# A transformer block on one core: order of the Q/K/V stage's x hand-over, halos, weight loads and first LN2 changed

## The chip, the cores and the metric

One Trainium2 chip, one core of it. The core has a matmul engine (TensorE, PE in the profile, with its weight loads as PEld), a vector engine (VectorE, DVE), a scalar engine (ScalarE, ACT), a general engine (GpSimd, POOL) and SyncE (SP), which here only issues DMAs. Each engine works through its own instructions in order and meets the others through semaphores. The metric is device time of one execution in microseconds (us). The kernel before took 362.25 us, the median of three executions (361.2 to 363.64).

## What is computed

A pre-LayerNorm block on x of 2048 rows by 576 columns, in bf16:

```python
qkv = LN(x) @ wqkv                      # 32 heads of 18 columns
logits[s, w] = q[s] . k[s - 2 w] / sqrt(18)      # w = 0..7, masked where s < 2 w
o = sum_w softmax(logits)[s, w] * v[s - 2 w]
h = x + o @ wo
out = h + gelu(LN(h) @ w1 + b1) @ w2 + b2        # w1: 576 x 4608, w2: 4608 x 576
```

## The kernel before

The 2048 rows are 16 tiles of 128; row `16 p + j` lies in tile j on partition p. So the rows that attention needs (2, 4, ... rows back) lie in tiles of the same parity on the same partition, and, where a tile number would fall under 0, in a tile of that parity one partition further down. All K and V of a parity stand in one ring, `kv_ring[parity]`, one slot a tile. Tiles are attended in falling order (`ATT_ORDER`, in the code `A`: 14, 12, ..., 0, 15, 13, ..., 1). When tile j has been attended to, its slot is replaced by the same tile moved down one partition, for the tiles that come after: `store_halo` (L306) writes the slot to `kv_dram`, `halo(j, 1)` (K) and `halo(j, 2)` (V, both L347) read it back moved. `halo(j, 1)` must follow the QK products of j and precede those of the next tile; `halo(j, 2)` does the same for the products with V.

The order of the work on PE, ACT, DVE, SP and POOL is written out by hand: what the Python code emits first, an engine does first.

**The Q/K/V stage, 24 visits.** `seq` lists 48 duos (tile, K or V or Q); visit `qd` takes duos 2 qd and 2 qd + 1. A duo (`qkv_duo`, matmuls at L228) runs in two phases, since each matmul uses half the array's rows and two run side by side: 10 matmuls in the first, 8 in the second. `visit` runs the first phase of every duo, then a hook, then the second phases, each followed by the duo's evacuation on ACT (L322) and by what `between` lists. Before a second phase starts, a no-op on POOL (`marker`, L238) must have seen the end of that duo's first phase. The duos use three PSUM buffers in turn (A, B, C), so a duo's first matmul waits for the evacuation of the duo three before. A fourth, D, serves the transposes and the duos with Wo. After each visit come `after[qd]` and `loads[qd]`. Visits 0 to 11 do K, Q and V of the even tiles, whose x is transposed on PE (`tr_x`); visits 12 to 23 do the odd tiles O0 to O7 (1, 3, ..., 15), three visits for a pair: V12 is K and V of O0, V13 Q of O0 and K of O1, V14 V and Q of O1, and so on; V21 is the first that reads the last pair, O6 and O7.

**x of the odd tiles** goes by DRAM. `ln1_act` (L174, ACT) normalizes a tile into `q_all`; `out_x(i)` (L292, L293, SP) stores pair i to `xd`; `in_x(i)` (L296, SP) reads it back transposed into `xnT`. A buffer of `xnT` (5 in all) is used again once the visits that read it are done.

**Attention of the first two tiles** (A[0] = 14, A[1] = 12) runs on DVE beside these visits: `att_qk_a` (L352: products), `att_qk_add` (L361: four folding adds), L368 to L375 (logits, maximum), `att_exp` on ACT, `att_den`, `att_pv` (L401 to L414), which leaves o in `q_all`. `o_tail` (L199, ACT) copies its last 64 columns twice, `tr_o` transposes it on PE (L182) into D, ACT copies it to `oT` (L434), and `wo_duo` multiplies by Wo as a third duo of a visit (`wo_with`). Then LN2: `ln2` adds x and takes statistics (L473, L148, L149, L155, L487, DVE), `ln2_rstd` raises to the power -0.5 (L161, POOL), `ln2_norm` (L539, L174, ACT) normalizes, `tr_h` transposes on PE (L188, L192), and ACT copies into `hnT` (L557). With both tiles in `hnT`, the MLP of group 0 starts.

**The MLP, 8 groups of two tiles.** For each group PE does `hn @ w1` (`pm`, L228, gelu on ACT, L584), Wo of the next group (`pw`), and the product with w2 (`po`, L603 for groups 0 and 1, L691 for the rest). Beside it DVE does attention and ACT and POOL LN2 of the next group. In group 0, attention of A[2] and A[3] is finished, `pv_t` sends o through DRAM (L210, L211, and the transposing read L216) to `oT`, and Wo of A[3] runs as a visit inserted at row 19 of the first w2 tile.

**Weight loads** (`load`, L104) wait for the last ACT evacuation before them (`pace`). `load_w1(c)` is a sixth of W1 (768 KB), `load_wo([q])` a quarter of Wo, `load_w2(n)` 3, 4 or 7 of W2's 36 row blocks of 144 KB. All go through SP's queue, in which an instruction that waits holds up those behind it; the loads' queue places are therefore set by the visit at which they are listed.

**Start.** 13 matmuls on constants (`busy`, L833) keep PE at work while the first x tile comes; then `tr_x` of the first tile and visit 0.

Of the kernel before, what the change touches and what calls it, by code (L numbers as in the profile page):

```python
# [17 lines left out]
def kernel(  # L18
# [12 lines left out]
    nc = tc.nc  # L31
    P = 128
    _, S, D = A_x.shape
# [57 lines left out]
    b2_bc = x_all[:, ODD[-1], :]  # L91
# [4 lines left out]
    def psum_pair(tag, name, dtype=F32):  # L96
        n = 512 if dtype == F32 else 1024
        return psum.tile([P, 2, n], dtype, tag=f"ps{tag}", name=name)
# [119 lines left out]
    def half_rows(r):  # L218
        return slice(r * HP, (r + 1) * HP)
# [51 lines left out]
    def new_xnT(js):  # L271
        t = qp.tile([P, KT, 2 * P], BF16, tag="xnT", name="xnT", bufs=5)
        for n, j in enumerate(js):
            xnT[j] = t[:, :, n * P:(n + 1) * P]
        return t

    def tr_x(j, tag):
        pair = psum_pair(tag or "CAB"[(ring_pos[0] + 1) % 3], "xt_pt")
        transpose_in(pair, q_all[:, j, :])
        if EVEN.index(j) % 2 == 0:  # L280
            new_xnT(EVEN[EVEN.index(j):][:2])
        for k0, k1 in ((0, 2), (2, KT)) if j in EVEN[0:2] else ((0, KT),):
            nc.scalar.copy(**turned(xnT[j], pair, k0, k1))
# [57 lines left out]
    def logit_of(js):  # L341
        return logits[:, sides(js)]
# [15 lines left out]
    def att_qk_add(j, steps):  # L358
        for o, a, c in steps:
            n = (c - a if c < 9 else 9) * H  # L360
            nc.vector.tensor_tensor(out=prod[:, :, o * H:o * H + n], in0=prod[:, :, a * H:a * H + n],  # L361
                                    in1=prod[:, :, c * H:c * H + n], op=ALU.add)

    def att_qk_b(j, i, skip=0):
        side[j] = i
        out = logit_of([j])[:, 0]
        att_qk_add(j, ((0, 0, 9), (0, 0, 4), (0, 0, 2), (0, 0, 1))[skip:])
        nc.vector.tensor_tensor(out=out, in0=prod[:, :, 0:H], in1=prod[:, :, 8 * H:9 * H], op=ALU.add)  # L368
        if j // 2 + 1 < W:
            nc.vector.memset(out[0:1, j // 2 + 1:W, :], -1e9)  # L370
# [332 lines left out]
    def c_(fn, *a):  # L703
        return lambda: fn(*a)
# [96 lines left out]
    def call(fns):  # L801
        for fn in fns:
            fn()

    with tc.manual_schedule(engines={ENG.PE, ENG.Activation, ENG.DVE, ENG.SP, ENG.Pool}):
# [23 lines left out]
        load_w1h()  # L829
        busy = psum_pair("D", "busy")  # L830
        ones = nc.const_aps.tensor(1.0, [P, 512], BF16)
        for n in [512] * 8 + [P] * 5:
            nc.tensor.matmul(busy[:, 0, 0:n], lhsT=ones[:, 0:P], rhs=ones[:, 0:n], start=True, stop=True)  # L833
        nc.gpsimd.memset(mhalf[:], -0.5)
        nc.gpsimd.memset(eps2[:], EPS * EPS)
# [63 lines left out]
        A = ATT_ORDER  # L899
# [35 lines left out]
            ln2_ins(c, d)  # L935

        loads = {}
        for c, v in enumerate((2, 3, 4, 13, 13, 17)):
            loads[v] = loads.get(v, []) + [c_(load_w1, c)]
        for q, v in enumerate((6, 8, 11, 12)):  # L940
            loads[v] = [c_(load_wo, [q])]
        for n, v in enumerate((19, 19, 20, 20, 21, 22)):
            loads[v] = loads.get(v, []) + [c_(load_w2, n)]
        after = {
            0: [c_(ln1_even, 3), c_(ln1_even, 4)],
            1: [c_(ln1_even_rstd, 2, 3), c_(ln1_even, 5)],
# [6 lines left out]
            8: [c_(att_qk_a, A[1]), c_(att_qk_rest, A[1], 1), c_(ln1_act, 8, 3), c_(out_x, 1),  # L953
                c_(store_halo, A[1]), c_(store_halo, A[0], slice(1, 2))],
            9: [c_(ln1_act, 9, 0)],
            10: [c_(att_pv, A[0]), c_(ln1_act, 9, 1), c_(in_x, 1), c_(halo, A[1], 1)],
            11: [c_(out_x, 2), c_(halo, A[0], 2)],
            12: [c_(ln1_act, 10, 0)],
            13: [c_(ln1_act, 10, 1), c_(in_x, 2), c_(out_x, 3), c_(store_halo, A[2]), c_(store_halo, A[3])],
            14: [c_(att_pv, A[1]), c_(in_x, 3), c_(load, b2_bc, B_b2.partition_broadcast(P))],  # L960
            15: [c_(halo, A[1], 2), c_(o_tail, A[0])],
            17: [c_(o_tail, A[1]), c_(ln2, A[0]), c_(att_qk_a, A[2])],
            18: [c_(ln2_rstd, A[0]), c_(halo, A[2], 1)],
            19: [c_(ln2, A[1])],
            20: [c_(ln2_rstd, A[1]), c_(att_qk_rest, A[2], 0)],
        }
        between = {
            10: [c_(att_exp, A[0])],
            13: [c_(att_exp, A[1])],
            18: {1: [c_(tr_o, A[1], "D")]},  # L970
            19: {1: [c_(ln2_norm, A[0])]},
            21: [c_(ln2_norm, A[1])],
            22: [c_(att_exp, A[2])],
        }
        wo_with = {17: A[0], 19: A[1]}
        hooks = {
            0: {1: lambda: call([c_(tr_x, EVEN[1], "C"), c_(ln1_even, 2)])},
            **{n: {m: c_(tr_x, EVEN[2 * n + m - 1], "D" if m == 1 else None) for m in (1, 2)} for n in (1, 2, 3)},
            12: c_(tr_b1, "D"),
            16: c_(tr_o, A[0], "D"),  # L980
            21: c_(tr_h, A[0], "D"),
            22: c_(tr_h, A[1], "D"),
        }
        seq = [(j, t) for t in (1, 2) for j in EVEN[:2]] + [(j, 1) for j in EVEN[2:]] \
            + [(j, 0) for j in A[0:2]] + [(j, 2) for j in EVEN[2:]] + [(j, 0) for n in (0, 4, 2) for j in EVEN[n:n + 2]] \
# [1 line left out]

        ln1_even_rstd(0, 1)
        tr_x(EVEN[0], "D")
        for qd in range(len(seq) // 2):  # L990
            duos = [qkv_duo(*seq[2 * qd]), qkv_duo(*seq[2 * qd + 1])]
            if qd in wo_with:
                duos.append(wo_duo(wo_with[qd], "D"))
            visit(duos, hooks.get(qd), between.get(qd, ()), apart=qd == 0)
            call(after.get(qd, ()))
            call(loads.get(qd, ()))
# [34 lines left out]
        p, q, r, s = "ABDC"  # L1031

        gelu_table()
        for k, g in enumerate(GROUPS):
            c, d = GROUPS[k + 1] if k + 1 < len(GROUPS) else (None, None)
# [87 lines left out]
            if 3 <= k < 7:  # L1123
                mlp2_fast(g, rows, (s, p, q, r), wo, x, True)
                p, q, r, s = q, r, p, s
            else:
                mlp2_fast(g, rows, (q, p, r, s), wo, x)
                p, q, r, s = r, s, p, q
# [30 lines left out]
```

## Time and profile before

| | |
|---|---|
| median of three executions | 362.25 us (361.2 to 363.64) |
| the profiled execution, its own time | 362.23 us |
| its span, first to last instruction | 360.4 us |
| PE / DVE / ACT / POOL busy | 352.6 / 295.9 / 235.9 / 48.1 us |
| mean granted TensorE clock | 0.995 |

| stretch, us from the span's start | what | PE busy | DVE busy | ACT busy |
|---|---|---|---|---|
| 0 to 35.80 | start, visits 0 to 11 | 33.28 | 30.23 | 27.33 |
| 35.80 to 68.15 | visits 12 to 23 | 30.33 | 30.62 | 21.85 |
| 68.15 to 106.31 | MLP group 0 | 38.16 | 34.33 | 29.08 |
| 106.31 to 144.12 | MLP group 1 | 37.81 | 35.93 | 24.13 |
| 144.12 to 323.60 | MLP groups 2 to 6 | 179.48 | 155.02 | 118.77 |
| 323.60 to 360.40 | MLP group 7, last stores | 33.50 | 9.73 | 14.74 |

How to read it: a timeline line gives start, duration, engine, source line, operation, what is written from what, count, and in brackets the idle time of that engine ahead of it with what ended the wait. Starts of neighbouring instructions can overlap, since an engine takes up the next one before the last has drained. The DMA column of a page gives no times on an engine: SP's lines are the issue of a DMA, and its landing comes later.

### The profile page before, as it was taken

What the parts mean: (1) busy time and instruction counts of PE and PEld (TensorE: products, weight loads), DVE (VectorE), ACT (ScalarE), POOL (GpSimd) and SP (SyncE); (2) the same over time, 40 slices, a digit from 0 to 9 for tenths busy, and PEclk for the clock granted to TensorE, in tenths of its full rate; (3) what the DMA queues carried; (4) which work ended last, traced back from release to release, by engine and by line L of the source; (5) the groups of instructions that cost most, each with busy time, mean ns of one, the idle gap of its engine ahead of it and who ended that gap; (6) DMA issues with size and microseconds to landing.
All of it is one profiled execution on the core that took longest, in us unless ns stands there. A gap on an engine that the chain in (4) does not pass through costs nothing.

```text
span 360.4 us, 11550 instructions
## 1 busy us (share of the span) xinstructions
PE 352.6 (98%) x4938; PEld 290.7 (81%) x4938; DVE 295.9 (82%) x416; ACT 235.9 (65%) x524; POOL 48.1 (13%) x61
## 2 busy tenths in 40 slices
PE   7999998999999999999999999999999999999996
PEld 3788886788778877887788778877887788778874
DVE  5999999989889998998799899989998989520431
ACT  4889764898556783668656956695669566706620
POOL 2340005000212020201110202021102110210000
PEclk8999999999999999999999999999999999999999
DMA  7996599972636496732463355344545254283001
GB/s 240 329 294 193 147 258 310 367 253 55 169 66 100 132 244 109 129 79 51 91 102 90 85 124 84 90 86 120 88 90 99 58 85 58 54 120 51 4 1 34
DMA packets 63492, 46.29 MB, mean 128 GB/s; under 512 B 32192, under 2 KB 61760, under 8 KB 63440
## 3 DMA queue, kind: packets, MB, share of 16 engines
q1 hardware_dynamic: 59472, 41.50, 43.6%
q0 software_dynamic: 3744, 3.84, 9.9%
q8 instruction: 38, 0.62, 0.8%
q10 hardware_dynamic: 224, 0.22, 0.3%
q14 instruction: 14, 0.11, 0.1%
HBM read 23.38 MB, written 12.42 MB: 99 GB/s over the span
## 4 chain that ended last, share of the span: by engine, by line
PE 80%; DVE 11%; DMA 5%; ACT 2%; issue 1%; SPq 0%; DVEq 0%; ACTq 0%
PE pm L228 39%; PE po L691 25%; PE po L603 10%; PE pw L228 4%; DMA xnT<-xd 3%; DVE ln_stats L148 2%; DVE prod L361 2%; DVE prod L407 1%; DVE prod L352 1%; PE pq L228 1%; DMA x_all<-in_A_x_dram 1%; DMA wq_sb<-in_A_wqkv_dram 1%; ACT h_all L584 1%; DVE prod L413 1%; DVE ln_mv L149 1%
## 5 line engine op out<-in xcount | busy, mean ns | idle before, releaser
L228 PE MATMUL pm<-hnT,w_sb 64*128 64x256 bf16 x2304 | 143.0, 269 | 0.0
L584 ACT ACTIVATE h_all<-pm,b_sb 128x256 f16<-128x256 f32 (+1 forms) x288 | 108.7, 496 | 51.0 <-PE pm L228 50.3
L228 PEld LDWEIGHTS <-w_sb 64*128 64x128 bf16 x2304 | 111.6, 94 | 15.2 <-issue 1.7
L228 PE MATMUL pq<-wq_sb,xnT 64*128 64x288 bf16 x720 | 55.7, 286 | 3.0 <-DMA xnT<-xd 1.8
L691 PEld LDWEIGHTS <-h_all 128*128 128x128 f16 x480 | 46.2, 98 | 13.7 <-issue 1.6
L228 PEld LDWEIGHTS <-xnT 64*128 64x128 bf16 x864 | 44.7, 95 | 11.9 <-DMA xnT<-xd 2.1
L361 DVE TENSOR_TENSOR prod<-prod 128x2304 bf16<-128x2304 bf16 (+1 forms) x64 | 44.2, 691 | 2.1
L352 DVE TENSOR_TENSOR prod<-kv_ring,q_all 128x4608 bf16<-128x4608 bf16 x16 | 40.8, 2551 | 3.2 <-POOL ln_rstd L498 2.4
L407 DVE TENSOR_TENSOR prod<-kv_ring,probs 128x4608 bf16<-128x4608 bf16 x16 | 40.9, 2558 | 2.2 <-DMA kv_ring<-kv_dram 1.7
L228 PE MATMUL pm<-hnT,w1h_sb 64*128 64x256 bf16 x288 | 39.2, 269 | 0.0
L691 PE MATMUL po<-w2a_sb,h_all 128*128 128x288 bf16 (+1 forms) x262 | 35.9, 286 | 0.0
L413 DVE TENSOR_TENSOR prod<-prod 128x2304 bf16<-128x2304 bf16 (+1 forms) x32 | 33.9, 1058 | 1.1
L603 PEld LDWEIGHTS <-h_all 128*128 128x128 bf16 x288 | 27.9, 98 | 7.9 <-issue 0.9
L691 PEld LDWEIGHTS <-kv_ring 128*128 128x128 f16 x252 | 24.6, 98 | 6.3
L603 PE MATMUL po<-w2a_sb,h_all 128*128 128x288 bf16 x224 | 28.5, 286 | 0.0
L228 PE MATMUL pq<-wqh_sb,xnT 64*128 64x288 bf16 x144 | 28.1, 288 | 0.0
L793 POOL DMA_DIRECT2D x_all<-o_sb x12 | 10.7, 888 | 125.1 <-PE pw L228 72.3
L498 POOL TENSOR_TENSOR ln_rstd<-ln_var,mhalf 128x1 f32<-128x1 f32 x13 | 10.2, 786 | 84.2 <-ACT ln_var L497 84.2
L161 POOL TENSOR_TENSOR ln_rstd<-ln_veps,mhalf 128x1 f32<-128x1 f32 (+2 forms) x14 | 14.1, 1019 | 45.4 <-DVE ln_nmean L487 28.0
L691 PE MATMUL po<-w2b_sb,h_all 128*128 128x288 bf16 (+1 forms) x122 | 19.7, 286 | 0.2 <-DVE h_all L671 0.2
L228 PE MATMUL pw<-wo_sb,oT 64*128 64x288 bf16 x256 | 19.5, 283 | 0.0
L671 DVE TENSOR_TENSOR kv_ring<-h_all 128x1536 f16<-128x1536 f16 (+3 forms) x9 | 6.8, 760 | 15.4 <-ACT h_all L584 15.3
(113 smaller groups left out, 400.3 us busy)
## 6 DMA issues: line engine op xcount, KB each, us to landing
w_sb<-in_B_w_dram SPq DMA_DIRECT2D x6, 768.0 KB, 6.3
kv_ring<-kv_dram SPq DMA_DIRECT2D x28, 144.0 KB, 2.4
kv_dram<-kv_ring SPq DMA_DIRECT2D x13, 288.0 KB, 4.3
x_all<-in_B_b_dram SPq DMA_DIRECT2D x15, 144.0 KB, 3.8
w2a_sb<-in_B_w_dram SPq DMA_DIRECT2D x2, 1008.0 KB, 7.1
td<-q_all SPq DMA_DIRECT2D x14, 144.0 KB, 2.3
td<-hn SPq DMA_DIRECT2D x14, 144.0 KB, 1.8
x_all<-h POOLq DMA_DIRECT2D x14, 144.0 KB, 4.5
```

Of the source, the lines that this page charges most:

```text
L148: nc.vector.bn_stats(out=stats[:, i, c, :], in_=src[:, c * HALF:(c + 1) * HALF])
L161: nc.gpsimd.tensor_tensor(out=rstd[:], in0=veps[:], in1=mhalf[:].to_broadcast([P, n]), op=ALU.pow)
L228: last = nc.tensor.matmul(duo["g"][r ^ swap][i], lhsT=lhsT, rhs=rhs, start=(swap == 0 and i == 0 and kt == 0), stop=(swap == 1 and kt == K ...
L352: ins = nc.vector.tensor_tensor(out=prod[:], in0=k_ring[j % 2], in1=q_all[:, j, :].unsqueeze(1) .to_broadcast([P, W, D]), op=ALU.mult).ins
L361: nc.vector.tensor_tensor(out=prod[:, :, o * H:o * H + n], in0=prod[:, :, a * H:a * H + n], in1=prod[:, :, c * H:c * H + n], op=ALU.add)
L407: nc.vector.tensor_tensor(out=prod[:].rearrange("p w (d h) -> p w d h", h=H), in0=v_ring[j % 2].rearrange("p w (d h) -> p w d h", h=H), in ...
L413: nc.vector.tensor_tensor(out=prod[:, 0:n, :], in0=prod[:, 0:n, :], in1=prod[:, n:2 * n, :], op=ALU.add)
L498: ins = nc.gpsimd.tensor_tensor(out=rstd[:], in0=var[:], in1=mhalf[:], op=ALU.pow).ins
L584: pace[0] = nc.scalar.activation(out=hT(grp)[:, f, 0:N], in_=ps[:, r, i * N:(i + 1) * N], func=ACT.Gelu_apprx_tanh, bias=b1_sb[:, f:f + 1] ...
L603: nc.tensor.matmul(banks[half], lhsT=hT(grp)[:, f, i * P:(i + 1) * P], rhs=w2_rows(f)[:, half * HALF:(half + 1) * HALF], start=(f == 0), s ...
L691: nc.tensor.matmul(bank, lhsT=l, rhs=r, start=start, stop=stop, skip_group_check=True)
L793: nc.gpsimd.dma_start(out=x_of(j), in_=o_of.pop(j), accum_op=ALU.add)
```

## The change

Nothing of the computation changes; the work per engine is the same but for 15 more matmuls on constants, and the order of these pieces is other:

```diff
-        for n in [512] * 8 + [P] * 5:
+        for n in [512] * 8 + [P] * 8:
             nc.tensor.matmul(busy[:, 0, 0:n], lhsT=ones[:, 0:P], rhs=ones[:, 0:n], start=True, stop=True)
...
-        for c, v in enumerate((2, 3, 4, 13, 13, 17)):
-            loads[v] = loads.get(v, []) + [c_(load_w1, c)]
-        for q, v in enumerate((6, 8, 11, 12)):
-            loads[v] = [c_(load_wo, [q])]
-        for n, v in enumerate((19, 19, 20, 20, 21, 22)):
-            loads[v] = loads.get(v, []) + [c_(load_w2, n)]
+        for v, fns in ((2, [(load_w1, 0)]), (3, [(load_w1, 1)]), (4, [(load_w1, 2)]), (6, [(load_wo, [0, 1])]), (8, [(load_wo, [2])]),
+                       (11, [(load_wo, [3])]), (14, [(load_w1, 4), (load_w1, 5)]), (15, [(load_w2, 0)]), (16, [(load_w2, 1)]),
+                       (17, [(load_w2, 2)]), (18, [(load_w2, 3)]), (20, [(load_w2, 4)]), (21, [(load_w2, 5)])):
+            loads[v] = [c_(*fn) for fn in fns]
...
-            10: [c_(att_pv, A[0]), c_(ln1_act, 9, 1), c_(in_x, 1), c_(halo, A[1], 1)],
-            11: [c_(out_x, 2), c_(halo, A[0], 2)],
-            12: [c_(ln1_act, 10, 0)],
-            13: [c_(ln1_act, 10, 1), c_(in_x, 2), c_(out_x, 3), c_(store_halo, A[2]), c_(store_halo, A[3])],
-            14: [c_(att_pv, A[1]), c_(in_x, 3), c_(load, b2_bc, B_b2.partition_broadcast(P))],
-            15: [c_(halo, A[1], 2), c_(o_tail, A[0])],
-            17: [c_(o_tail, A[1]), c_(ln2, A[0]), c_(att_qk_a, A[2])],
-            18: [c_(ln2_rstd, A[0]), c_(halo, A[2], 1)],
-            19: [c_(ln2, A[1])],
-            20: [c_(ln2_rstd, A[1]), c_(att_qk_rest, A[2], 0)],
+            10: [c_(att_pv, A[0]), c_(ln1_act, 9, 1), c_(out_x, 2), c_(in_x, 1), c_(halo, A[1], 1), c_(load_w1, 3)],
+            11: [c_(ln1_act, 10, 0)],
+            12: [c_(ln1_act, 10, 1), c_(out_x, 3), c_(in_x, 2)],
+            13: [c_(halo, A[0], 2), c_(in_x, 3), c_(store_halo, A[2]), c_(store_halo, A[3])],
+            14: [c_(att_pv, A[1]), c_(load, b2_bc, B_b2.partition_broadcast(P))],
+            15: [c_(o_tail, A[0])],
+            16: [c_(halo, A[1], 2)],
+            17: [c_(ln2, A[0]), c_(att_qk_a, A[2])],
+            18: [c_(att_qk_add, A[2], ADDS[:2])],
+            19: [c_(halo, A[2], 1)],
+            20: [c_(ln2, A[1]), c_(att_qk_rest, A[2], 0, 2)],
...
         between = {
...
-            18: {1: [c_(tr_o, A[1], "D")]},
-            19: {1: [c_(ln2_norm, A[0])]},
-            21: [c_(ln2_norm, A[1])],
+            18: [c_(o_tail, A[1])],
+            19: {0: [c_(ln2_rstd, A[0])], 1: [c_(ln2_norm, A[0])]},
+            21: {0: [c_(ln2_rstd, A[1])], 1: [c_(ln2_norm, A[1])]},
...
-        wo_with = {17: A[0], 19: A[1]}
+        wo_with = {17: A[0], 20: A[1]}
...
-            21: c_(tr_h, A[0], "D"),
-            22: c_(tr_h, A[1], "D"),
+            19: c_(tr_o, A[1], "D"),
+            22: c_(tr_h, A[0], "D"),
+            23: c_(tr_h, A[1], "D"),
...
         tr_x(EVEN[0], "D")
+        busy = psum_pair("B", "busy")
+        for n in range(12):
+            sl = half_rows(n % 2)
+            nc.tensor.matmul(busy[:, n % 2, 0:P], lhsT=ones[sl, 0:P], rhs=ones[sl, 0:P], start=True, stop=True)
```

`ADDS` is the list of the four folding adds of `att_qk_add`. In words: the last odd pair's x is normalized after V11 and V12 (before: V12 and V13), stored after V12 (V13) and read after V13 (V14), and both come ahead of the V halo of A[0] or of the two K/V stores where they stood behind them. Of W1, sixth 3 moves from V13 to V10, sixth 4 from V13 to V14 and sixth 5 from V17 to V14. W2's six pieces move from V19 to V22 to V15 to V21, so that four of them stand ahead of the K halo of A[2] in SP's queue. Of Wo, quarter 1 moves from V8 to V6, 2 from V11 to V8, 3 from V12 to V11. The transposes of o of A[1] move from the end of V18 to the middle of V19, its Wo duo from V19 to V20, its LN2 statistics from after V19 to after V20, and DVE does two of A[2]'s folding adds ahead of them. The two LN2 powers on POOL are emitted behind the markers of V19 and V21 (before: ahead of them). The transposes of h move from V21 and V22 to V22 and V23.

More of the change, by code (lines that the diff above doesn't have):

```diff
@@ L362, in att_qk_add @@
                                     in1=prod[:, :, c * H:c * H + n], op=ALU.add)
+    ADDS = ((0, 0, 9), (0, 0, 4), (0, 0, 2), (0, 0, 1))
     def att_qk_b(j, i, skip=0):
@@ L366, in att_qk_b @@
         out = logit_of([j])[:, 0]
-        att_qk_add(j, ((0, 0, 9), (0, 0, 4), (0, 0, 2), (0, 0, 1))[skip:])
+        att_qk_add(j, ADDS[skip:])
         nc.vector.tensor_tensor(out=out, in0=prod[:, :, 0:H], in1=prod[:, :, 8 * H:9 * H], op=ALU.add)
```

## The prediction

> **What bounds the kernel now.** First the page's busy line: PE is busy for 352.6 of 360.4 us, so all that can be won is in its few waits.
>
> ```profile
> PE 352.6 (98%) x4938; PEld 290.7 (81%) x4938; DVE 295.9 (82%) x416; ACT 235.9 (65%) x524; POOL 48.1 (13%) x61
> ```
>
> Then PE's waits, whole span: nothing of size after the Q/K/V stage, and one large wait in it.
>
> ```profile
> PE pq L228 <- DMA xnT<-xd: 1.8, 1, 1.8
> PE pq L228 <- DMA wq_sb<-in_A_wqkv_dram: 1.1, 2, 0.7
> ```
>
> Its place is in the chain of waits (start, us, what): the read of the last pair, issued at 51.01, landed only at 60.40, and V21 needs it at 58.5. Behind it the chain goes over LN2 of A[1]: V22's `tr_h` waits for hn.
>
> ```profile
> 51.01 9.39 DMA xnT<-xd
> ...
> 60.44 1.40 PE pq L228 x20
> ...
> 63.64 0.88 ACT hn L174
> ...
> 64.56 0.29 PE h_pt L188 x8
> ```
>
> Third, the timeline around the two hand-overs of o to PE. Here DVE, not PE, sets the pace: o of A[0] is ready at 45.51, its tail copy at 45.84, and PE comes at 45.90. For A[1] PE has finished at 52.53 and starts at 52.85.
>
> ```profile
> 45.05 0.46 DVE L414 TENSOR_TENSOR q_all<-prod 128x576 bf16<-128x576 bf16 x1
> ...
> 45.54 0.30 ACT L199 COPY tail<-q_all 128x128 bf16<-128x128 bf16 x1
> ...
> 45.90 0.28 PE L182 MATMUL o_pt<-ident,q_all 64*128 64x64 bf16 x8
> ```
>
> Fourth, the granted clock (us, busy of PE, PEld, DVE, ACT, POOL, clock, DMA): PE runs at half clock from 6.93 to 10.33.
>
> ```profile
> 3.52:6.93 3.41, 1.78 (x25) 1.07 (x24) 2.67 (x10) 1.53 (x4) 0.56 (x2) 1.00 0.98 319
> 58.13:61.54 3.41, 1.66 (x28) 1.12 (x25) 3.20 (x9) 1.29 (x3) 1.66 (x1) 1.00 1.06 351
> 6.93:10.33 3.40, 3.29 (x38) 1.85 (x35) 2.71 (x8) 1.50 (x3) 0.52 (x1) 0.50 1.08 351
> ```
>
> Last, DVE's and POOL's timeline. DVE has no gap from 24 us to 63 us; then it waits twice for a halo, and PE meets DVE's product again at 91.80, where Wo of A[3] needs oT.
>
> ```profile
> 63.60 2.56 DVE L352 TENSOR_TENSOR prod<-kv_ring,q_all 128x4608 bf16<-128x4608 bf16 x1 [0.47 <-DMA kv_ring<-kv_dram]
> ```
> ```profile
> 79.77 2.56 DVE L407 TENSOR_TENSOR prod<-kv_ring,probs 128x4608 bf16<-128x4608 bf16 x1 [0.97 <-DMA kv_ring<-kv_dram]
> ```
> ```profile
> 91.80 0.48 PEld L228 LDWEIGHTS <-oT 64*128 64x128 bf16 x10 [0.24 <-DMA oT<-td]
> ```
> ```profile
> 54.17 2.86 POOL L161 TENSOR_TENSOR ln_rstd<-ln_veps,mhalf 128x1 f32<-128x1 f32 x1 [26.38 <-DVE ln_nmean L487]
> 58.65 1.66 POOL L161 TENSOR_TENSOR ln_rstd<-ln_veps,mhalf 128x1 f32<-128x1 f32 x1 [1.62 <-DVE ln_nmean L487]
> ```
>
> **Part 1, constants at the start.** The first run of `busy` ends at 4.30 and PE then waits until 4.83: three more of 128 columns cost a quarter of a 512-column one each (0.43 us apart), 0.11, so 0.32 in a gap of 0.53. The twelve run in six pairs, 0.64 us at half clock, in the gap from 5.15 to 5.87. Cost 0; were both gaps gone, 0.96. They may keep the clock up. A stretch with 1.78 us PE busy of 3.41 lost the clock, one with 1.66 kept it; but the first holds many short transposes whose drain counts as busy. Streaming alone I estimate at 1.2 us for it (0.6 `busy`, 0.13 transposes, 0.48 pq) and 1.5 for the second. With 15 more, at least 0.16 + 0.32 = 0.48 at full clock, the first has 1.7, so I take the clock as kept: 3.4 x 0.5 = 1.7 us sooner on PE at 10.33. That goes into a wait: V16 meets o of A[0] at 45.90, which is DVE's chain, without a gap since 24 us and before that bound to x. Worth 0 on the path (ends: 0 and 1.7).
> The Trainium skill (TensorE: Matmul & The Clock Gate, Part 1) lets the clock fall only after an idle window of about 3.4 us. The 3.40 us at half clock agree in length; that the window before was half busy does not. By that rule the 15 matmuls would change nothing, and the sum would be the same.
>
> **Part 2, x of the last pair.** On ACT two `ln1_act` (0.87 each) go one visit earlier. The first now stands ahead of V12's evacuations, so V13's second duo waits about 0.1 at 38.7, inside the meeting with DVE. `out_x(3)` issues at about 40.4 instead of 46.63. `halo(A0, 2)` waits for DVE until 42.79 and now no longer holds up the last quarter of Wo, `out_x(3)` and `in_x(2)`, only `in_x(3)`, which issues at about 44.1 when its store has landed (3 us). It lands by 48 at 3.7 us, the median of these four, by 54 at its old 9.39; needed at 58.2. So 58.51 to 60.44, 1.93 us, goes whole. `in_x(1)` is pushed behind `out_x(2)` to about 37.1, lands at 40.8, needed at 42.5. The K/V stores (4.2 us) are needed at 56.6 only.
>
> **Part 3, A[1] a visit on.** A visit takes 2.20 us (first phases at 18.79, 20.99, 23.20), a Wo duo 1.10, `tr_o` 0.14, `tr_h` 0.38. `tr_o` in the middle of V19 falls at 53.75, after o (52.13) and the tail (52.46): the 0.32 us at 52.53 goes. Then V20 starts at 54.88, with Wo until 58.2, V21 58.2, V22 60.5. DVE does two folding adds first (1.37 + 0.70), so LN2 of A[1] runs from 58.62, not 56.53, its last result comes at 60.7. Total DVE work until 63.12 is unchanged.
> The powers behind the markers: before, V19's first marker stood behind a power until 54.13, needed at 54.83. Worth 0 (ends 0 and 0.1, the marker's lateness against its need if PE comes sooner). Now V20's and V22's markers stand behind the powers, but are not needed before 56.7 and 62.1, and the powers can start at 54.17 and 60.7. What is new is ACT's order: norm of A[1], hnT of A[0], V22's evacuations. The power of A[1] starts at 60.7. Its price is unknown: spans of 2.86, 1.66 and 0.67 (at 91.67), longer the longer the DVE operation beside it (2.48, 1.37, 0.42). Beside it now are adds of 0.43 and 0.30: I take 0.8, between 0.67 and 1.66 but nearest the 0.67. Then 61.5; nmean and hn 1.2, 62.7; hnT 0.65; V22's first evacuation 0.6, 63.95. V23's second duo wants that buffer at 63.7: waits 0.3. `tr_h` of A[1] in V23 then finds hn ready (0.29 of the old wait gone). V21's second duo waits 0.1 for an evacuation behind norm of A[0].
> PE reaches the MLP at 68.15 - 0.32 - 1.93 - 0.29 + 0.3 + 0.1 = 66.0, 2.1 us sooner. With a power of 1.66 it is 1.2; with 2.86, 0.1.
>
> **Part 4, loads and halos.** W2's first four pieces, W1's last two, b2 and two stores, 4.5 MB, are now queued between 45.5 and 53.6, ahead of `halo(A2, 1)` at 56.6. At the 260 to 380 GB/s that the windows of 5 us from 50 to 70 show they take 12 to 17 us: with 0.4 for itself the halo lands at 59 (it cannot before, at 2.4 after issue) to 63 instead of 63.58, DVE wants it at 63.12: 0.47 won. Behind the waiting halos in SP's queue stand W2's second piece (`halo(A1, 2)`, until 49.5) and its last two (`halo(A2, 1)`, until 56.6), which are not used before 87 us: 0. W1's sixth 3, now at about 39, shares the engines with `in_x(1)` and `out_x(3)`; W1's fourth and fifth are used behind 72, and come sooner or as soon. Wo's quarters come two or three visits sooner and are used at 48.25: 0. The V halo of A[2], issued at 74.79 behind W2's last pieces, took 4.88; those pieces are now through by about 73, so it takes some 2.4 (page: median) and 0.97 is won. DVE comes 1.44 sooner. oT of A[3]: transposed read issued at 88.74 plus 2.92 is 91.66, so now 90.2; PE wants it at 91.80 - 2.1 = 89.7. It waits 0.5. (If the store ahead of that read took 2.6 as its twin and not 3.66, no wait.)
>
> **Sum.** 2.1 - 0.5 = 1.6 us. From 92 us on DVE waits for PE again (0.87 at 93.82), all chains shift together, PE has no waits: it reaches the end. 362.23 - 1.6 = 360.6 for the profiled execution, which is 0.02 from the median.
>
> **Rivals.** Clock too: if DVE's chain also came sooner, the 1.7 us would reach the end: 360.6 - 1.7 = 358.9. Against it: DVE has no gap in which PE could speed it up. Chance 0.1.
> Nothing left: the power is caught by longer DVE work or ACT's row at V22 is slower than I hold, and V23 gives all back: 2.1 - 2.0 = 0.1 won, 362.1. For it: the rows of 2.86 and 1.66. Chance 0.2.
> Slower, the K halo of A[2] behind W2: if it lands as late as w2b did (9.85 after issue), at 66.5, DVE is 2.9 later there, less 0.97 later on, and oT of A[3] comes at 93.6: 1.8 late, 364.0. It decides from a landing at about 64.7. For it: four W2 pieces now ahead of it; against: 1 to 4 us of slack at the rates seen. Chance 0.15.
> A rule speaks for it: in the Trainium skill (DMA: Bandwidth & Descriptors, Queues, rings and completion order) each DMA engine takes one queue's descriptors in ring order, so the halo cannot pass W2. The trace agrees: 6.93 us for that halo behind W1's last sixth, against a median of 2.4.
>
> **How the numbers follow.** 360.6 has 0.55; its own range is 360.1 (store as its twin) to 361.4 (power 1.66, halo late by little). The range takes in both other sides, 358.7 to 363.4, leaving part of the slower case out. About 1% (3.6 us) is what a measurement of this kernel can tell from no change; no case but mishaps of two rivals together passes it. Faster by over 1%: 0.06, slower 0.05, within 0.89.
>
> **What would show it.** Gone: PE's wait for xnT from xd. New: PE waits at V16's transposes of o by up to 1.6 us (clock 1.00 between 6.93 and 10.33), in V23 by some 0.3, before Wo of A[3] by some 0.5. First `pm` at about 66.0; DVE's waits for kv_ring gone. A power of A[1] over 1.7, a halo landing after 63.1, or a new PE wait between 10 and 45 beyond DVE's would make it wrong.

## The result, and the profile after

| | before | after |
|---|---|---|
| median on the same chip | 361.83 us (360.79 to 363.64, 8 runs) | 364.54 us (363.92 to 365.49, 8 runs) |
| the profiled execution, its own time and span | 362.23, 360.4 | 365.49, 363.5 |
| first `pm` of the MLP | 68.15 | 70.56 |

The change is slower, by less than 1%: ratio 1.0076, 95% interval 1.0054 to 1.0099, that is 2.7 us (2.0 to 3.6). The forecast was 360.6 in a range of 358.7 to 363.4.

The page's busy line after: PE is again busy for 98% of the span, but the span and PE's busy time both grew by about 3 us.

```profile
PE 355.5 (98%) x4953; PEld 292.1 (80%) x4953; DVE 296.0 (81%) x416; ACT 236.1 (65%) x524; POOL 47.2 (13%) x61
```

PE's waits, whole span (total, times, longest). The 1.8 us at V21 for `xnT` are gone. (So are the waits for `wq_sb`, but those come and go between executions: run 3 below, with the same start, has one of 0.5 us.) In their place stands the transpose of o of A[1]; "DVE h" is only what came last by the profile, the wait is for DVE's chain ahead of it.

```profile
PE o_pt L182 <- DVE h L475: 2.6, 1, 2.6
...
PE pw L228 <- DMA oT<-td: 0.4, 1, 0.4
PE pq L228 <- DMA xnT<-xd: 0.3, 1, 0.3
```

The same view for DVE names the cause: a halo, in a product with V.

```profile
DVE prod L409 <- DMA kv_ring<-kv_dram: 4.5, 3, 4.1
```

DVE's timeline shows both products that read a late ring (lines 407 and up of before are two higher here). The first waits 4.14 us; before, it started with no wait (first line). The second is the one that waited 0.47 at 63.60 before; it now starts at 67.71 without a wait, which looks harmless and is not, as the experiments show.

```profile
46.89 2.56 DVE L407 TENSOR_TENSOR prod<-kv_ring,probs 128x4608 bf16<-128x4608 bf16 x1
```
```profile
51.02 2.56 DVE L409 TENSOR_TENSOR prod<-kv_ring,probs 128x4608 bf16<-128x4608 bf16 x1 [4.14 <-DMA kv_ring<-kv_dram]
...
67.71 2.55 DVE L352 TENSOR_TENSOR prod<-kv_ring,q_all 128x4608 bf16<-128x4608 bf16 x1
```

SP's timeline tells why the halo is late. Before, `halo(A0, 2)` was issued at 42.79 and the read of pair 2 (`xnT<-xd`) stood behind it and took 1.40 us to issue. Before, too, one such read took long: that of the last pair, 3.86 us, behind two sixths of W1 issued from 48.84 on.

```profile
42.79 0.34 SPq L347 DMA_DIRECT2D kv_ring<-kv_dram  x1
...
45.18 1.40 SPq L296 DMA_TRANSPOSE xnT<-xd  x1
...
51.01 3.86 SPq L296 DMA_TRANSPOSE xnT<-xd  x1
```

After, W1's sixth 3 (first line) goes ahead of the read of pair 2, which takes 3.60 us to issue, and `halo(A0, 2)` stands behind it: it is issued at 46.51.

```profile
39.28 0.43 SPq L104 DMA_DIRECT2D w_sb<-in_B_w_dram  x1
...
42.82 3.60 SPq L296 DMA_TRANSPOSE xnT<-xd  x1
46.51 0.54 SPq L347 DMA_DIRECT2D kv_ring<-kv_dram  x1
```

The chain of waits then runs from that halo (4.42 us to land, 2.46 before) over the product to PE's transpose at 56.98, which came at 52.85 before.

```profile
46.51 4.42 DMA kv_ring<-kv_dram
...
51.02 2.57 DVE prod L409
...
56.98 0.32 PE o_pt L182 x10
```

Last, the granted clock by windows (us, busy of PE, PEld, DVE, ACT, POOL, clock, DMA share, GB/s). PE's wait of 2.6 us is followed by 3.41 us at half clock, so by another 1.7 us lost. The stretch at half clock at 6.93 is absent in this execution.

```profile
54.58:57.99 3.41, 1.01 (x25) 1.04 (x27) 3.27 (x7) 1.50 (x4) 0.00 (x0) 1.00 0.95 279
57.99:61.40 3.41, 3.41 (x34) 2.68 (x30) 3.34 (x5) 1.35 (x4) 2.86 (x1) 0.50 1.07 386
```

So the MLP's start adds up: 68.15, less the three waits that went as forecast (0.32 + 1.93 + 0.29 = 2.54), plus 0.35 at V18 (pair 2's x), 2.61 at the transpose and 1.7 for the clock, is 70.3; measured 70.56.

That is the account of the profiled execution, the slowest of the eight. The half clock is not in all of them: a stretch of 3.41 us at half clock makes the mean clock of a span of 363.5 us 0.995, and only two of the eight have 0.995 (365.49 and 365.15 us), the others 0.999 or 1.0 (363.92 to 365.09). So the 1.7 us are no part of the 2.7 us between the medians. What is, the experiments show.

### The profile page after: what moved, and what is told of

It reads as the page before. It is cut to its first block, busy times and chain, and to the rows that moved or that the text cites. A ratio compares the mean times of both kernels' runs of the same rounds, so it can differ in the third digit from the quotient of the medians.

```text
span 363.5 us, 11584 instructions
## 1 busy us (share of the span) xinstructions
PE 355.5 (98%) x4953; PEld 292.1 (80%) x4953; DVE 296.0 (81%) x416; ACT 236.1 (65%) x524; POOL 47.2 (13%) x61
## 4 chain that ended last, share of the span: by engine, by line
PE 81%; DVE 12%; DMA 3%; SPq 1%; ACT 1%; issue 1%; DVEq 0%; ACTq 0%
PE pm L228 38%; PE po L693 25%; PE po L605 10%; PE pw L228 5%; PE pq L228 3%; DVE ln_stats L148 2%; DVE prod L361 2%; DVE prod L409 1%; DVE prod L352 1%; DMA x_all<-in_A_x_dram 1%; DMA kv_ring<-kv_dram 1%; DVE prod L415 1%; ACT h_all L586 1%; SPq L104 1%; DMA oT<-td 1%; DVE ln_mv L149 1%
## 5 line engine op out<-in xcount | busy, mean ns | idle before, releaser
L352 DVE TENSOR_TENSOR prod<-kv_ring,q_all 128x4608 bf16<-128x4608 bf16 x16 | 40.8, 2550 | 2.8 <-POOL ln_rstd L500 2.5
L161 POOL TENSOR_TENSOR ln_rstd<-ln_veps,mhalf 128x1 f32<-128x1 f32 (+2 forms) x14 | 13.1, 950 | 52.2 <-DVE ln_nmean L489 34.7
```

The costliest lines, as they stand in the source:

```text
L161: nc.gpsimd.tensor_tensor(out=rstd[:], in0=veps[:], in1=mhalf[:].to_broadcast([P, n]), op=ALU.pow)
L352: ins = nc.vector.tensor_tensor(out=prod[:], in0=k_ring[j % 2], in1=q_all[:, j, :].unsqueeze(1) .to_broadcast([P, W, D]), op=ALU.mult).ins
```

## The experiments

**The theory.** Two halos became late, and they stand in series on DVE. The first is the V halo of A[0], behind the read of pair 2 in SP's queue. The second is the K halo of A[2], behind four pieces of W2. Each by itself takes all that the change wins, and in the changed kernel the first hides the second: `halo(A2, 1)` must wait for A[2]'s products on DVE, so a late first halo makes the second late as well (it is issued at 60.76, before at 56.64) and DVE comes late to it too. Rivals: one of them is the whole cost; the constants cost something; the shift of A[1] is what hurts. (The product that waits for the K halo of A[2] is that of A[3], L352; the expectations call it A[2]'s.) All were timed beside the kernel before on one chip for each group of four; before had 361.67, 361.41 and 361.59.

**1. The V halo ahead of the read of pair 2**

```diff
-            12: [c_(ln1_act, 10, 1), c_(out_x, 3), c_(in_x, 2)],
-            13: [c_(halo, A[0], 2), c_(in_x, 3), ...
+            12: [c_(ln1_act, 10, 1), c_(out_x, 3), c_(halo, A[0], 2), c_(in_x, 2)],
+            13: [c_(in_x, 3), ...
```

> The changed kernel with one edit: the V halo of A[0] stands in SP's queue behind the store of the last x pair and ahead of in_x(2), not behind in_x(2). Theory: the loss is DVE's 4.1 us wait for this halo, which in the changed kernel was issued at 46.51 instead of 42.79 since in_x(2)'s issue ahead of it took 3.6 us. Then here it issues at 42.9, lands by 47.3 at the latest, DVE waits under 0.5 us, PE's 2.6 us wait at tr_o of A[1] and the half clock in V19 and V20 go; in_x(2) lands some 0.5 later (V18 waits up to 0.9): 361.0 us. Rival 1, the shift of A[1]'s Wo, LN2 and transposes by a visit is what costs: 363 or more, since that stays. Rival 2, it is the load on the DMA engines (W1's sixth 3 beside the halo) and not the queue: the halo still lands after 49, DVE still waits over 2 us, 363.

Measured: 364.69, ratio 1.0076 (1.0047 to 1.0104): no better than the change. Yet the halo is issued at 42.43, the 4.1 us are gone, and the first `pm` comes at 66.28, as the forecast had it. DVE's timeline shows where the time went: the second halo. A[2]'s products end at 56.98, but SP is at W2's pieces until 59.93, one of which takes 3.89 us to issue, so that halo is issued at 60.03 and lands 7.6 us later.

```profile
47.26 2.56 DVE L409 TENSOR_TENSOR prod<-kv_ring,probs 128x4608 bf16<-128x4608 bf16 x1 [0.76 <-DMA kv_ring<-kv_dram]
...
67.67 2.56 DVE L352 TENSOR_TENSOR prod<-kv_ring,q_all 128x4608 bf16<-128x4608 bf16 x1 [4.16 <-DMA kv_ring<-kv_dram]
```

PE's waits show who pays: Wo of A[2], which starts 18.67 us after A[3]'s products.

```profile
PE pw L228 <- DMA oT<-td: 2.0, 1, 2.0
```

**2. W1's sixth 3 behind V14 instead of V10**

```diff
-            10: [..., c_(halo, A[1], 1), c_(load_w1, 3)],
+            10: [..., c_(halo, A[1], 1)],
...
-                       ... (14, [(load_w1, 4), (load_w1, 5)]), ...
+                       ... (14, [(load_w1, 3), (load_w1, 4), (load_w1, 5)]), ...
```

> The changed kernel with one edit: W1's sixth 3 is loaded after V14 with the next two, not after V10; the halo stays behind in_x(2). If in_x(2)'s issue of 3.6 us comes from W1's sixth filling the engines ahead of it, it takes 1.4 us here, the halo issues at 44.3 and lands at 46.7, DVE waits not at all or 0.2, in_x(2) lands by 47 and V18 does not wait: 360.6 us. If the issue is long by itself (queue order alone): halo at 46.5, DVE waits 2 to 4 us, 364.

Measured: 363.27, ratio 1.0052 (1.0032 to 1.0072). SP's timeline: with no W1 sixth on the engines the same read takes 1.34 us to issue, and the halo behind it is in time although the order is that of the change.

```profile
41.93 1.34 SPq L296 DMA_TRANSPOSE xnT<-xd  x1
43.31 0.58 SPq L347 DMA_DIRECT2D kv_ring<-kv_dram  x1
```

The first halo is cured, `pm` starts at 65.74, and the 360.6 us of the forecast do not come: again DVE waits for the K halo, here 3.06 us until 66.03.

**3. Both cures of the first halo**

> Both edits of the two kernels before together. Theory of the late halo: no DVE wait, no PE wait in V18 or V19, clock full: what the prediction said of the rest, 360.5 us, and no better than the W1 edit alone. Rival (A[1]'s shift costs by itself): 362 or more, with a PE wait between V19 and the MLP.

Measured: 364.07, ratio 1.0065 (1.0042 to 1.0088), `pm` at 66.87; DVE waits 3.6 us for the K halo (landed 67.64), PE 2.1 at Wo of A[2], and then runs 3.41 us at half clock from 86.46 (four of the ten executions have a mean clock of 0.994 or 0.995, and 364.83 to 365.51 us; the six others 363.15 to 364.48). Curing the first halo twice is worth no more than once.

**4. The change without the 15 matmuls on constants**

> The changed kernel without the 15 matmuls on constants (5 of 128 columns at the start as before, none of the twelve). Theory: half clock from about 7 to 10.3 us again, PE 1.7 us later at V16, where it no longer waits for o of A[0]; DVE's wait for the halo and all behind it as in the changed kernel: 364.5 us, within 0.4. Rival: the constants set the phase of what follows or let PE run into its own waits, and are the loss: 362.

Measured: 364.56, ratio 1.0076 (1.005 to 1.0101), the same as with them. Its profiled execution has full clock at the start without them, which the forecast did not expect, and both halo waits side by side (3.4 and 2.2 us).

**5 to 7. W2's pieces back at V19 to V22, with each state of the first halo**

```diff
-  ... (15, [(load_w2, 0)]), (16, [(load_w2, 1)]), (17, [(load_w2, 2)]), (18, [(load_w2, 3)]), (20, [(load_w2, 4)]), (21, [(load_w2, 5)]) ...
+  ... (19, [(load_w2, 0), (load_w2, 1)]), (20, [(load_w2, 2), (load_w2, 3)]), (21, [(load_w2, 4)]), (22, [(load_w2, 5)]) ...
```

The fifth has the edit of the first besides, the sixth that of the second, the seventh nothing else.

> The changed kernel with the V halo of A[0] issued ahead of the read of pair 2, and W2's six pieces back at the visits of the kernel before, behind the K halo of A[2]. Theory (two late halos, each enough by itself to cost what the change gains): both DVE waits go; the 4.1 us ahead of the products with V as with the halo alone, and the 4.2 us ahead of A[2]'s products with K to 0.5 or less, since four W2 pieces less stand before that halo and it lands by 63.5. The first pm starts at 66.0 to 66.5, PE waits at most 0.6 at Wo of A[3], and the time is 360.0 to 361.0, faster than both kernels. Rival (DVE's sum of work sets oT of A[3], the halos only show where it waits): the wait at Wo of A[3] stays near 2 us and the time is 362 or more. Second rival (W2 later is needed by the second product of the MLP): PE waits for w2a or w2b, 362 or more.

> The changed kernel with sixth 3 of W1 back behind V14 and W2's six pieces at the visits of the kernel before. It cures the V halo in the other way (no load fills the engines while the read of pair 2 is issued, 1.34 us instead of 3.60) and the K halo of A[2] as in the twin with the halo moved ahead. Theory of two late halos: pm starts at 65.7 to 66.3, the wait of 3.1 us ahead of A[2]'s products with K falls to 0.6 or less, time 359.8 to 360.8. Rival (DVE's sum of work sets oT of A[3]): 362 or more, a wait of about 2 us at Wo of A[3] stays.

> The changed kernel with only W2's six pieces back at the visits of the kernel before; the V halo of A[0] stays behind the read of pair 2. Theory (two late halos in series on DVE, the first hides the second): DVE's wait ahead of the products with V stays 3.5 to 4.5 us, pm starts at 69 to 70.5, DVE comes to A[2]'s products with K too late to meet that halo, and the time stays within 0.8 of the changed kernel, 363.5 to 364.6. Rival (W2 early is the whole cost): 361 or less with pm at 66 to 67.

Measured: 361.29 (ratio 0.9997, 0.9977 to 1.0018), 361.03 (0.9984, 0.9963 to 1.0005) and 363.46 (1.0053, 1.0025 to 1.0081). W2 alone does not cure it, either cure of the first halo alone does not, both together bring the time back to that of the kernel before (both intervals contain 1). These are all the waits that the view lists for PE in the sixth's span of 358.8 us:

```profile
PE busy L835 <- PEq L1149: 0.8, 1, 0.8
PE pq L228 <- ACT kv_ring L322: 0.7, 1, 0.7
PE pq L228 <- DMA xnT<-xd: 0.2, 1, 0.2
PE po L693 <- DVE h_all L673: 0.2, 1, 0.2
```

Its DVE reaches A[3]'s product at 63.45 with no wait; before it was 63.60 with one of 0.47. The fifth and the sixth came out slower than forecast (360.0 to 361.0 and 359.8 to 360.8). In the fifth, whose profiled execution is the slowest of its twelve, W1's sixth 3 still goes ahead of the V halo and the read: the V halo is issued at 43.46 and DVE waits for it 1.76 us, until 49.12; the read of pair 2 takes 2.90 us to issue, PE waits 1.4 us for x (in two places), and `pm` starts at 68.15. The seventh keeps the first wait, as theory had it:

```profile
50.24 2.56 DVE L409 TENSOR_TENSOR prod<-kv_ring,probs 128x4608 bf16<-128x4608 bf16 x1 [3.92 <-DMA kv_ring<-kv_dram]
```

What this wait costs in the end depends on the clock. PE waits 2.4 us for o of A[1], as in after, and the profiled execution then runs 3.41 us at half clock. Four of the ten executions have a mean clock of 0.994 or 0.995 (which does not say where the stretch lies) and take 363.83 to 364.47 us; of the six with 0.999 or 1.0, five take 361.42 to 363.09, one 364.98. So with full clock the first halo alone costs about 0.8 us against before (median 362.2 of the six, an estimate from few executions), and with the half clock some 2.7.

**8. The kernel before, with W2 early and nothing else**

```diff
-        for n, v in enumerate((19, 19, 20, 20, 21, 22)):
+        for n, v in enumerate((15, 16, 17, 18, 20, 21)):
```

> The kernel before with one part of the change alone: W2's six pieces at V15, V16, V17, V18, V20 and V21. Nothing else moves. Theory: the K halo of A[2], issued at about 57 to 58, now stands behind W1's last sixth and four W2 pieces and lands at 66 to 67.5 instead of 63.58; DVE's wait ahead of A[2]'s products with K grows from 0.47 to 2.5 to 4 us, and PE, which comes to Wo of A[3] at 91.8, waits there 1.5 to 3 us: 363.3 to 365. The first pm stays at 68 to 68.3. Rival (the halo passes W2, or its delay is taken up by DVE's later slack): 361.5 to 362.3 as before.

Measured: 364.30, ratio 1.0085 (1.0055 to 1.0115). This is the forecast's slower rival made alone, with three pieces of W2 ahead of the halo, not four, since `halo(A2, 1)` stands a visit sooner here than in the change. The halo lands 3.1 us later than before, about half of it because SP is held up at the loads ahead of it (issued at 58.09, not at 56.64) and half because it takes longer to land (8.57 us, not 6.93). In this execution `pm` starts at 66.40, 1.75 sooner than in that of before (the read of the last pair landed at 57.71, not at 60.40, so V21 did not wait at all), which I had not expected; and still the end comes 2 us later. The clock adds to it: two of the seven executions keep it (0.999 and 1.0) and take 363.3 us, the five others 363.54 to 366.11. DVE's timeline, PE's timeline and the clock:

```profile
66.69 2.56 DVE L352 TENSOR_TENSOR prod<-kv_ring,q_all 128x4608 bf16<-128x4608 bf16 x1 [3.39 <-DMA kv_ring<-kv_dram]
```
```profile
85.34 1.08 PE L228 MATMUL pw<-wo_sb,oT 64*128 64x288 bf16 x8 [1.96 <-DMA oT<-td]
```
```profile
82.04:85.45 3.41, 1.45 (x28) 1.15 (x24) 3.38 (x2) 2.90 (x8) 0.00 (x0) 1.00 0.24 49
85.45:88.86 3.41, 3.41 (x32) 2.32 (x31) 3.34 (x6) 0.57 (x3) 0.00 (x0) 0.50 0.34 96
```

The chain of the same execution shows the way from the product to Wo: A[2]'s o stands behind A[3]'s products on DVE (66.69 to 80.56), then come a store and a transposing read.

```profile
75.31 2.57 DVE prod L407
...
80.97 1.57 DMA td<-q_all
...
82.55 2.75 DMA oT<-td
...
85.34 1.32 PE pw L228 x10
```

**9. The kernel before, with x of the last pair early alone, the V halo ahead of the read of pair 2**

```diff
-            11: [c_(out_x, 2), c_(halo, A[0], 2)],
-            12: [c_(ln1_act, 10, 0)],
-            13: [c_(ln1_act, 10, 1), c_(in_x, 2), c_(out_x, 3), ...
-            14: [c_(att_pv, A[1]), c_(in_x, 3), ...
+            11: [c_(ln1_act, 10, 0)],
+            12: [c_(ln1_act, 10, 1), c_(out_x, 3), c_(halo, A[0], 2), c_(in_x, 2)],
+            13: [c_(in_x, 3), ...
+            14: [c_(att_pv, A[1]), ...
```

(`out_x(2)` stands at V10, as in the change.)

> The kernel before with x of the last pair alone made, stored and read a visit earlier as in the change, but with the V halo of A[0] left ahead of the read of pair 2; all weight loads, A[1], LN2 and the constants as before. Theory (x early wins what PE waited at V21, about 1.9 us in the profiled execution of the kernel before, if no halo is made late by it): the read of the last pair is issued at 45 to 48 us instead of 51.01, PE's wait of 1.8 us at V21 is gone, the first pm starts at 66.5 to 67.5 since the tr_h of A[1] still waits for hn, and the time is 360.0 to 361.2. Rival (V21 was only where DVE's chain showed, so LN2 of A[1] and oT of A[3] hold PE instead): pm at 67.5 to 68.3 and the time within 0.5 of the kernel before. Second rival (the read goes in front of W1's sixths and shifts them, so a halo is late again): a DVE wait for kv_ring over 2 us and 362.5 or more.

Measured: 360.95, ratio 0.9987 (0.9973 to 1.0002), span 358.8. The wait at V21 is gone, `pm` starts at 66.12, sooner than the 66.5 expected. (Both are nearly so in run 8 as well, which leaves x where it was; this run alone does not show that the move of x did it.) PE's waits, but for that of `busy` at the start:

```profile
...
PE pq L228 <- ACT xnT L283: 0.5, 1, 0.5
PE pw L228 <- DMA oT<-td: 0.2, 1, 0.2
```

**10. The sixth without the constants**

> The changed kernel with W1's sixth 3 and all of W2 later, as run before at 361.03, and without the 15 added matmuls on constants. Theory (the constants are worth nothing, since V16 waits for o of A[0] whatever PE's clock was at 10 us): within 0.5 of the twin with the constants, 360.6 to 361.5, also where the clock is halved near 7 us. Rival (they keep the clock and the 1.7 us reaches the end): 362.2 or more whenever the clock is halved at the start.

Measured: 360.55, ratio 0.9982 (0.9963 to 1.0001). Its profiled execution does lose the clock, from 7.44 on, and DVE still starts its first product with V at 40.06 (39.87 with the constants): as the forecast's first part has it, nothing of it reaches the path.

**11. The kernel before, with the third part alone** (A[1] a visit on, with it `halo(A1, 2)` and `halo(A2, 1)`, LN2's powers behind the markers; all loads, x and the constants as before)

> The kernel before with the third part of the change alone: o of A[1] transposed in the middle of V19, its Wo duo in V20, LN2 behind two folding adds of A[2], the powers behind the markers, the transposes of h in V22 and V23. x, all loads and the constants as before. Theory (this part only takes away two small waits of PE, 0.3 us each, and V21 still waits for x): the time is within 0.8 of the kernel before, 360.8 to 362.0. Rival (the later LN2 of A[1] makes tr_h of V23 wait, 1 us or more): 362.5 or more with a PE wait for hn before the first pm.

Measured: 361.15, ratio 0.9986 (0.9964 to 1.0007). It does no harm. PE waits 0.66 us at V21 for x, not 1.75 as in the profiled execution of before.

**12. The kernel before, with the first halo made late**

```diff
-        for c, v in enumerate((2, 3, 4, 13, 13, 17)):
+        for c, v in enumerate((2, 3, 4, 10, 13, 17)):
...
-            11: [c_(out_x, 2), c_(halo, A[0], 2)],
-            12: [c_(ln1_act, 10, 0)],
-            13: [c_(ln1_act, 10, 1), c_(in_x, 2), c_(out_x, 3), ...
+            11: [c_(out_x, 2)],
+            12: [c_(ln1_act, 10, 0), c_(in_x, 2)],
+            13: [c_(ln1_act, 10, 1), c_(halo, A[0], 2), c_(out_x, 3), ...
```

> The kernel before with one thing alone made late: the read of pair 2 goes ahead of the V halo of A[0] in the queue, and W1's sixth 3 is loaded behind V10, as in the change; x of the last pair, A[1], LN2, W2 and the constants as before. Theory (the V halo is late because the transposing read ahead of it takes 3 us or more to issue while a W1 sixth fills the engines): the halo lands at 48.5 to 51 instead of 45.24, DVE waits 2 to 4 us ahead of A[1]'s products with V, o of A[1] comes that much later to PE's transposes behind V18, and the time is 363 to 366. Rival (DVE's slack or V21's wait for x takes the delay up): 362.3 or less.

Measured: 367.38, ratio 1.0163 (1.013 to 1.0195). The wait is there, larger than expected, but not alone, so the price of the first halo by itself is not read from it. Here `out_x(2)` stands behind W1's sixth 3 and lands only at 46.40, the read waits for it until 46.71 (and then takes 1.33 us to issue), and the last quarter of Wo, behind both in the queue, is late too. DVE's timeline, and PE's waits:

```profile
53.04 2.56 DVE L407 TENSOR_TENSOR prod<-kv_ring,probs 128x4608 bf16<-128x4608 bf16 x1 [5.90 <-DMA kv_ring<-kv_dram]
```
```profile
PE pw L228 <- DMA wo_sb<-in_A_wo_dram: 3.8, 1, 3.8
```

**All executions in one rule.** PE comes to Wo of A[2] 16.71 us behind the first `pm` when nothing holds it (84.86 - 68.15 before). Its o is there at the earliest 18.65 us behind the start of A[3]'s products (85.34 - 66.69 in the eighth). The later of the two sums against the profiles, in us:

| | first `pm`, + 16.71 | A[3]'s products, + 18.65 | Wo of A[2] starts | span |
|---|---|---|---|---|
| before | 68.15, 84.86 | 63.60, 82.25 | 84.86 | 360.4 |
| after | 70.56, 87.27 | 67.71, 86.36 | 87.27 | 363.5 |
| 1, V halo first | 66.28, 82.99 | 67.67, 86.32 | 86.34 | 363.1 |
| 2, W1 later | 65.74, 82.45 | 66.03, 84.68 | 84.68 | 361.4 |
| 3, both cures | 66.87, 83.58 | 67.66, 86.31 | 86.40 | 363.5 |
| 4, no constants | 68.90, 85.61 | 68.31, 86.96 | 87.01 | 362.8 |
| 5, V halo first, W2 later | 68.15, 84.86 | 65.29, 83.94 | 84.85 | 361.0 |
| 6, W1 and W2 later | 66.31, 83.02 | 63.45, 82.10 | 83.01 | 358.8 |
| 7, W2 later | 69.79, 86.50 | 66.93, 85.58 | 86.49 | 362.6 |
| 8, before, W2 early | 66.40, 83.11 | 66.69, 85.34 | 85.34 | 362.5 |
| 9, before, x early | 66.12, 82.83 | 62.95, 81.60 | 83.30 | 358.8 |
| 10, 6 without constants | 66.68, 83.39 | 63.83, 82.48 | 83.62 | 359.1 |
| 11, before, third part | 67.05, 83.76 | 63.58, 82.23 | 84.46 | 359.9 |
| 12, before, V halo late | 73.23, 89.94 | 70.06, 88.71 | 90.36 | 365.8 |

The two constants come from the rows of before and of run 8, so these two fit by choice; eight others follow within 0.1. The last four rows start 0.2 to 0.7 later than the rule says: there the store of o takes 2.7 to 3.9 us where it took 1.8 in the eighth, so the 18.65 is a lower bound. From there to the end it is 275.4 to 276.8 us, and 277.1 and 277.2 in the third and the eighth, which have the half clock in it. That spread of over 1 us is not in the rule; in run 1 the stage behind Wo of A[2] has further waits (0.6 us for `hnT`, 0.3 for a marker) that are not there before.

In after the two sums lie 0.9 us apart: to cure the first halo alone can win no more than that. Run 4, which is the change without the constants and has full clock throughout, shows what decides then: DVE's 86.96 and not PE's 85.61. Six of the eight executions of after have full clock, so there DVE's chain, with both late halos in it, should set the time; no profile of such an execution was taken.

## Why the prediction was wrong, step by step

**The step that failed** is in its second part: "`halo(A0, 2)` waits for DVE until 42.79 and now no longer holds up the last quarter of Wo, `out_x(3)` and `in_x(2)`, only `in_x(3)`". It went through what the halo no longer delays, and never through what now delays the halo, nor who waits for it. A delay of this halo was put at nothing, without a reason. The read of pair 2 stands ahead of it, with W1's sixth 3 in flight (the fourth part says that this sixth shares the engines with other transfers, and gives no price), and DVE has 46.89 - 45.24 = 1.65 us of slack there. The halo came 3.72 us later to its issue and took 1.96 more to land; less the slack, 4.0: measured 4.14. A price could have been read from before: there the read of the last pair, behind two sixths, took 3.86 us to issue. The third part has the same hole from the other side: "`tr_o` in the middle of V19 falls at 53.75, after o (52.13)" takes o's time over from before.

**The second failure is a size**, in the fourth part: "the halo lands at 59 to 63 instead of 63.58 ... 0.47 won". It landed at 67.68, and with the V halo in time still at 67.64 and 66.01 (runs 1 and 2). The 12 to 17 us were about right for the queue (16.5 in after, from 51.19, when b2's load was issued; 18.8 in run 2, from 47.18, with W1's sixth 3 in the queue as well), but the start was not: the forecast counted from 45.5, and W2's pieces wait in SP's queue behind the halo that is late, the reads and the stores. It also kept the halo's issue at 56.6; SP was held up at W2's pieces and issued it at 60.03 and 58.37 in runs 1 and 2 (in after at 60.76, when the late products of A[2] had ended). The rival with this mechanism had 0.15, 364.0 and a threshold of 64.7. Runs 1, 2, 3 and 8 show the mechanism; by the rule above the threshold at `pm` of 66.0 is 66.0 + 16.71 - 18.65 = 64.1. Its place was wrong: the forecast had PE wait at Wo of A[3] (91.80), and PE waits 6.5 us sooner at Wo of A[2]. That the measured 364.54 lies near this rival's 364.0 is partly chance: its sum has neither the first halo nor this place. So two late halos, the first not seen at all, came together, and the range ended at 363.4.

The Trainium skill (DMA: Bandwidth & Descriptors, Queues, rings and completion order) says that each DMA engine takes one queue's descriptors in ring order; it says this of the order in which they are taken, not of the order in which transfers complete. Run 8 agrees: nothing but W2's pieces was moved ahead, and the halo took 8.57 us from issue to landing instead of 6.93. The forecast quoted it for the rival and gave it too little weight.

**What held, and what was luck.** Part 1: the constants are worth nothing (runs 4 and 10), as is the clock at 7 us. That they keep the clock up is not shown: all six executions of run 4 keep it without them, and of the 78 executions of before that were timed beside the experiments 66 have a mean clock of 0.998 or more (median 361.5 us; the 12 others 361.9).

Part 2: the wait at V21, 1.93 us in the forecast and its largest term, is gone in the changed kernel and in run 9. But it was large in one execution only. With x where it was before, run 8 has no wait there and run 11 one of 0.66 us. So what an earlier x wins in the usual execution is smaller than 1.93, and how much is not shown.

Part 3: the 0.32 and 0.29 go once the halo is in time, run 11 is harmless, and the power of A[1], taken as 0.8 between 0.67 and 1.66, is 0.73. POOL's timeline after:

```profile
65.42 0.73 POOL L161 TENSOR_TENSOR ln_rstd<-ln_veps,mhalf 128x1 f32<-128x1 f32 x1 [4.27 <-DVE ln_nmean L489]
```

The MLP's start, forecast at 66.0, is 65.74 and 66.31 in runs 2 and 6.

**The sum.** Run 6 is the change without late halos, but with W1's sixth 3 and W2 later: its span is 358.8, 1.6 below that of before, the forecast's 1.6 to the tenth. That is partly luck: the time of that same execution is 361.18, 1.05 below 362.23, and the run's median is only 0.4 us below (interval from 1.3 faster to 0.2 slower), that of run 9 0.6, of run 10 1.0. The profiled execution of before, 362.23, lay 0.4 to 0.8 above the medians of before; a sum made against it, with its long wait at V21, promises part of its own bad luck. Whether any of these versions is faster than before is left open: all three intervals end just above 1.

What stays open: how much the first halo would cost alone in the kernel before (run 12 mixes it with other late loads), and why a transposing read takes up to 3.6 us to issue while a W1 sixth is in flight. That the read of pair 2 is issued slowly behind the sixth and faster without it is shown (2.80 to 3.60 us in after and runs 1, 4, 5 and 7, 1.32 to 2.09 in the other nine kernels); what in the queue makes it so is not.

## What to carry to other kernels

For each transfer that the change moves, ask both questions: whom does it no longer hold up, and what does it now stand behind, with how much slack at its reader; a read ahead of it in the queue cost 3 us here, and the trace of before already held such a read. When a stage has two chains that meet (here PE's from the first `pm`, DVE's from A[3]'s products), write down both arrival times with their fixed distance to the meeting, since winning on one of them is worth only the gap to the other. A missing wait in the trace of a slow kernel proves nothing: in after the K halo is 4 us late and no engine waits for it, because another late halo stands before it. And before a single wait is made the largest term of a forecast, look for it in a second execution: the 1.75 us at V21 were 0 and 0.66 us in two other kernels with the same order of x.

## What the runs showed of the hardware

The issue of one and the same transposing read (`xnT<-xd`, pair 2) on SP took 1.32 to 2.09 us when no W1 sixth was in flight (before, runs 2, 3, 6 and 8 to 12; in run 12 the sixth had landed) and 2.80 to 3.60 us when one had been issued 3.5 to 4.4 us ahead (after, runs 1, 4, 5 and 7). All that stands behind it in SP's queue is late by as much. It is not the transposing alone: plain loads of W2 took between 0.38 (run 2) and 3.89 us (run 1) to issue in the same stage.

PE's clock fell to half for 3.41 us after single waits of 2.0 to 2.6 us (after, runs 3, 7 and 8), and for 6.83 us, from 51.57 on, in the middle of a wait of 3.8 us (run 12). At half clock 3.41 us cost 1.7, so such a wait costs nearly twice its length. The clock did not fall after waits of 2.0 us in the profiled executions of runs 1 and 2, and in run 7 four executions of ten have a mean clock that tells of such a fall. In the 3.41 us ahead of the fall PE was busy for 0.65 us (run 12), 0.96 (run 7), 1.01 (after), 1.28 (run 3) and 1.45 (run 8). The Trainium skill (TensorE: Matmul & The Clock Gate, Part 1) has a free-running window of about 3.4 us and calls the moment variable from run to run; the length and the variation agree with these rows, but here windows that were 19 to 43% busy lost the clock, where the page asks for an idle one.
